# One chunk of w4 loaded by two DMA engines instead of sixteen, in a decode step that streams its cache

## The chip, the cores and the metric

The kernel runs on one core of a Trainium2 chip. The core has TensorE (PE; its weight loads are listed as PEld), VectorE (DVE), ScalarE (ACT), GpSimd (POOL) and SyncE (SP), and sixteen DMA engines that move data between HBM and SBUF, its on-chip memory of 128 partitions. Matmul results go to PSUM. The metric is the time of one execution on the device in microseconds (us); lower is better.

## The reference

Eight sequences, one new token each. Block A is attention over the last 2048 positions of a key and value cache, block B an MLP whose token-shift branch is zero for a sequence of length one:

```python
x = A_x                                                   # [8, 1, 512]
h = x + A(layernorm(x))          # q = x @ wq; softmax(q k^T / sqrt(128)) v; @ wo
# B(u), with u = layernorm(h):
#   x1 = u + 0                   # the shifted branch is zero here
#   B  = x1 + gelu(layernorm(x1) @ w3) @ w4               # w3 [512, 1792], w4 [1792, 512]
h2 = h + B(layernorm(h))
```

There are 8 key-value heads of 128 elements and 32 query heads, all in bf16. Keys and values make 64 MB of the 79 MB that the kernel reads, wq and wo 4 MB each, w3 and w4 1.8 MB each.

## The kernel before

The instruction order of each engine is written out by hand. `Engine.op` appends an operation with the semaphores that it waits for, and `emit` writes the waits and the instructions. `dma` (line 197) appends a transfer; its semaphore gets 16 when the whole transfer has landed. All large loads are issued by SP, in one order: wq, then keys and values in 32 loads of 2 MB through a ring of eight buffers of 16 KB per partition, then wo in four parts, w3 in two, w4 in four. So each transfer stands behind all earlier ones in the queues of the DMA engines, and the order of issue is the order of arrival. A load of keys or values waits until TensorE has read the buffer that it overwrites.

w3 and w4 reuse two buffers of the ring (`w3_sb`, `w4_sb`). w3 goes as two loads of 256 rows with 7 KB per partition (line 669 on). w4's 1792 rows are 14 chunks of 128 rows (`FC = 14`); a chunk is what one matmul contracts over, and its 128 rows stand on the 128 partitions. The loop at line 675 loads 8, 3, 2 and 1 chunks with one DMA each, on four semaphores. In a DMA of r chunks, partition p gets r consecutive rows of 512 elements (r KB in one run), so chunk i of it holds rows `f0 + i`, `f0 + i + r`, and so on. The list `w4_chunks` keeps that as a slice with step r. The same slice picks the columns of w3 in `pe_w3` (line 705), so that row p of the product `y_ps` is what meets row p of w4's chunk. Its inner matmul (line 710) makes one chunk, 128 columns of w3, from one of four 128-row pieces (`kc`) of the contraction. Chunks 0 to 7 lie in one PSUM bank with 64 columns each, chunks 8 to 13 in another with 32 each.

The end of the kernel runs so. When the last part of wo has landed, TensorE finishes the attention's projection (line 548). VectorE and TensorE take the statistics of the layernorms (lines 685 to 700). `pe_w3` runs in two halves, each behind its half of w3. VectorE scales the product (line 738), ScalarE applies gelu (line 741). `pe_fin` (line 747) puts the residual into the output's PSUM tile, and `pe_w4` (line 755) adds w4's chunks, two matmuls per chunk, in four calls; each waits for its part of w4. Two copies (lines 775 and 776) take the result to SBUF, and SP stores it (line 779). `stream` (line 596) puts matmuls that nothing reads between these steps.

Of the kernel before, what the change touches and what calls it, by code (L numbers as in the profile page):

```python
# [12 lines left out]
D = 512  # L13
# [10 lines left out]
KC = D // 128  # L24
# [43 lines left out]
def bass_sequential_preLN__sliding_block_cached__mixer_s_mlp__decode_kernel(  # L68
# [23 lines left out]
    with es:  # L92
# [31 lines left out]
        w3_sb = ring[:, W3S, 0:KC * F].rearrange("p (k f) -> p k f", k=KC)  # L124
        w4_sb = ring[:, W4S, 0:FC * D].rearrange("p (k n) -> p k n", k=FC)
# [45 lines left out]
        uT = P4_sb[:, 0:64, :].rearrange("p (n w) k -> p n (w k)", n=KC)  # L171
# [22 lines left out]
        sem_w4 = [S(f"sem_w4{i}") for i in range(4)]  # L194
        PE, AC, DV, PO, SP = (Engine(S(n)) for n in ("s_pe", "s_act", "s_dve", "s_pool", "s_sp"))

        def dma(eng, dst, src, sem, *waits):
            def f(e):
                e.dma_start(dst, src).then_inc(sem, 16)  # L199
            eng.op(f, *waits, inc=False)  # L200
# [18 lines left out]
        e = DV.op(lambda e: e.bn_stats(st6[:, :], x_sb[:, :]), X)  # L219
        e = DV.op(lambda e: e.bn_aggr(mv[:, :], st6[:, :]), e)  # L220
        e = AC.op(lambda e: e.activation(rstd[:, :], mv[:, 1:2], ACT.Sqrt, bias=eps1[0:B, :], scale=1.0), e, e_eps)
        e = DV.op(lambda e: e.reciprocal(rstd[:, :], rstd[:, :]), e)
# [36 lines left out]
        e = PE.op(pe_xT, e_xln, e_idb)  # L259
# [22 lines left out]
        e = PE.op(pe_qT, *e_qr)  # L282
# [218 lines left out]
        cols = [slice(256 * a + r, 256 * (a + 1), 2) for a in range(2) for r in range(2)]  # L501
# [3 lines left out]
        def bc(t):  # L505
            a = t[:, :]
            return bass.AP(tensor=a.tensor, offset=a.offset, ap=[a.ap[0], [0, KC], [1, B]])
# [47 lines left out]
        at = {4 * (w + 1) + 2: w for w in range(SHARE)}  # L555
# [97 lines left out]
        for l in loads:  # L653
            what, b, j = l
            if what == "wo":
                n, qh = b, QH // NWO
# [4 lines left out]
            n = place[l]  # L661
# [6 lines left out]
        w_free = [taken[quads[n - NS]] for n in (len(quads), len(quads) + 1)]  # L668
# [2 lines left out]
                B_w3[256 * a:256 * (a + 1), :].rearrange("(p r) f -> p (r f)", r=2), sem, w_free[0])  # L671

        FH = 8
        w4_chunks, w4_ends, f0 = [], [], 0
        for r, sem in zip((8, 3, 2, 1), sem_w4):
            lo = len(w4_chunks)
            w4_chunks += [slice(f0 + i, f0 + 128 * r, r) for i in range(r)]
            dma(SP, w4_sb[:, lo:lo + r, :].rearrange("p r n -> p (r n)"),
                B_w4[f0:f0 + 128 * r, :].rearrange("(p r) n -> p (r n)", r=r), sem, w_free[1] if lo == 0 else None)
            w4_ends.append(lo + r)  # L680
            f0 += 128 * r
        assert len(w4_chunks) == FC
# [20 lines left out]
        y_ps, NY = [kbank[0], kbank[2]], (64, 32)  # L703

        def pe_w3(half, lo, hi, *waits):
            def f(e):
                for fc in range(lo, hi):
                    n, f = divmod(fc, FH)
                    for kc in (2 * half, 2 * half + 1):
                        ins = e.matmul(y_ps[n][:, f * NY[n]:(f + 1) * NY[n]], w3_sb[:, kc, w4_chunks[fc]],  # L710
                                       uT[:, kc, 0:NY[n]], start=(kc == 0 and f == 0), stop=(kc == KC - 1),
                                       skip_group_check=True)
                return ins
            return PE.op(f, *waits)
        pe_w3(0, 0, FC, e_u, (sem_w3[0], 16), e_scale[LAST, 1], e_acc[NV - 2])
# [3 lines left out]
        e = AC.op(lambda e: e.activation(s2[:, :], vsum[:, :], ACT.Sqrt, bias=eps2[:, :], scale=(1.0 + EPS) / D), e_vs)  # L719
# [3 lines left out]
        e = DV.op(lambda e: e.reciprocal(r1[:, :], s1[:, :]), e1)  # L723
        e = DV.op(lambda e: e.tensor_tensor(v3(xb[:, :]), v3(hc[:, :]), bc(r1), ALU.mult), e, e_hc)
        e = DV.op(lambda e: e.tensor_tensor(xb[:, :], xb[:, :], hp[:, :], ALU.add), e)
        e = DV.op(lambda e: e.tensor_tensor(v3(fin[:, :]), hT, v3(xb[:, :]), ALU.add), e)
        e = DV.op(lambda e: e.tensor_copy(f_hi[:, :], fin[:, :]), e)
        e_fin = DV.op(lambda e: e.tensor_tensor(f_lo[:, :], fin[:, :], f_hi[:, :], ALU.subtract), e)

        def bcf(t, n):  # L730
            a = t[:, :]
            return bass.AP(tensor=a.tensor, offset=a.offset, ap=[a.ap[0], [0, n], [1, B]])

        e_gT = []
        for n in range(2):
            fn = (FH, FC - FH)[n]
            cs = slice(n * FH * B, (n * FH + fn) * B)
            e = DV.op(lambda e, n=n, cs=cs, fn=fn: e.tensor_tensor(v3(g_x[:, cs]), 
                y_ps[n][:, 0:fn * NY[n]].rearrange("p (f w) -> p f w", w=NY[n])[:, :, 0:B], bcf(r2, fn),
                                                                   ALU.mult), e_y[n], e_r2)  # L740
# [10 lines left out]
        def pe_w4(lo, hi, *waits):  # L751
            def f(e):
                for fc in range(lo, hi):
                    for a in range(2):
                        ins = e.matmul(z_ps[64 * a:64 * a + B, 0:256], gT[:, fc * B:(fc + 1) * B],  # L755
                                       w4_sb[:, fc, 256 * a:256 * (a + 1)].rearrange("p (j r) -> p r j", r=2),
                                       start=False, stop=(fc == FC - 1), tile_position=(0, 64 * a), skip_group_check=True)
                return ins
            return PE.op(f, *waits)
# [7 lines left out]
        PE.op(pe_fin, e_fin, e_exp[LAST], e_scale[LAST, 1])  # L767
        stream(2)
        for n, hi in enumerate(w4_ends):
            e_z = pe_w4(w4_ends[n - 1] if n else 0, hi, (sem_w4[n], 16), e_gT[0 if hi <= FH else 1])  # L770
        e_out = []
        for a in range(2):
            src = z_ps[64 * a:64 * a + B, 0:256].rearrange("p (r j) -> p r j", r=2)
# [39 lines left out]
```

## Time and profile before

| | |
|---|---|
| median of 3 runs | 193.51 us (193.48 to 193.56) |
| profiled execution | 193.76 us, of which the span from first to last instruction is 192.3 us |
| busy share: PE, DVE, ACT, POOL | 83%, 54%, 44%, 19% |
| DMA traffic | 79.18 MB read from HBM, 412 GB/s over the span |
| loads issued by SP | 43: wq 4096 KB, 32 of 2048 KB, 4 of 1024 KB, 2 of 896 KB, and w4's 1024, 384, 256 and 128 KB |
| instruction loads | 16 of 16 KB on queue 8, beside a few of 8 KB on queue 14 |
| granted TensorE clock | full speed throughout |

The profile is of one execution. Its slices of the span give busy shares in tenths. The chain of waits is followed back from the last instruction, at each step to what released it. The table by window gives, for each engine, busy microseconds and the number of instructions, then the clock, the mean busy share of the DMA engines and what they moved. Beside the page, the trace holds the packets of the DMA engines with their queue, start, duration and size, and, for each load, the time of the increments that its semaphore took. It does not number the DMA engines. Times are counted from the start of the span.

### The profile page before, as it was taken

The page shows a single profiled execution, that of the slowest core. Times are in us where ns is not written, and L with a number is a line of the kernel's source. Part 1 is how long each engine was busy: PE and PEld are TensorE (multiplying, and loading weights), DVE is VectorE, ACT ScalarE, POOL GpSimd, SP SyncE. Part 2 cuts the span into 40 slices and gives each one's busy share as a digit, 9 for nine tenths or more (in the row PEclk, how much of TensorE's full clock was granted, in tenths as well). Part 3 has the DMA queues.
Part 4 walks back from the last instruction along what each step waited for, and adds up shares of the span by engine and source line. Part 5 has one row for each costly group of instructions (what it writes and reads, how often), then busy time and mean ns, then how long its engine had stood idle before and what let it go on. Part 6 is the DMA issues. An engine that isn't in the chain of part 4 may idle for free.

```text
span 192.3 us, 4741 instructions
## 1 busy us (share of the span) xinstructions
PE 159.8 (83%) x2108; PEld 101.8 (53%) x2108; DVE 103.8 (54%) x256; ACT 84.4 (44%) x102; POOL 35.8 (19%) x44
## 2 busy tenths in 40 slices
PE   0028999789998989998999797979998998898795
PEld 0015767567665555655656464646565653366472
DVE  7702656367457654665475546554765456552050
ACT  5002776946744544454444532454445423530040
POOL 8000000350520080008000800052004402400000
PEclk9999999999999999999999999999999999999999
DMA  6999999999999999999999999999999999999992
GB/s 220 436 423 436 433 416 433 426 428 423 436 429 433 429 433 423 426 429 431 433 423 433 429 433 429 429 433 426 424 426 429 429 433 433 423 416 430 418 381 77
DMA packets 6244, 79.47 MB, mean 413 GB/s; under 512 B 705, under 2 KB 849, under 8 KB 1361
## 3 DMA queue, kind: packets, MB, share of 16 engines
q1 hardware_dynamic: 6208, 79.18, 97.0%
q8 instruction: 16, 0.26, 0.5%
q10 hardware_dynamic: 16, 0.01, 0.0%
q14 instruction: 4, 0.02, 0.0%
HBM read 79.18 MB, written 0.01 MB: 412 GB/s over the span
## 4 chain that ended last, share of the span: by engine, by line
DMA 78%; PE 16%; DVE 2%; SPq 2%; issue 1%; ACT 0%
DMA ring<-in_A_k_cache_dram 63%; DMA ring<-in_B_w_dram 16%; PE kT_ps L325 8%; PE O_ps L445 3%; PE S_ps L345 3%; SPq L199 2%; DVE kT_sb L336 1%; PE sm L394 1%; PE sm L496 1%; DVE pT_sb L407 1%; PE S_ps L755 0%; DVE mcol L356 0%; ACT P_sb L775 0%; PE sm L360 0%; PE sm L370 0%
## 5 line engine op out<-in xcount | busy, mean ns | idle before, releaser
L334 ACT ACTIVATE kT_sb<-kT_ps 128x1024 bf16<-128x1024 bf16 x64 | 65.2, 1023 | 65.4 <-PE kT_ps L325 65.4
L325 PE MATMUL kT_ps<-ident_p,ring 128*128 128x128 bf16 x1024 | 68.3, 220 | 9.0 <-DMA ring<-in_A_k_cache_dram 7.6
L336 DVE COPY kT_sb<-kT_ps 128x1024 bf16<-128x1024 bf16 x64 | 44.3, 692 | 48.9 <-PE kT_ps L325 48.9
L325 PEld LDWEIGHTS kT_ps<-ident_p,ring 128*128 128x128 bf16 x1024 | 57.7, 98 | 22.5 <-DMA ring<-in_A_k_cache_dram 10.5
L384 POOL TENSOR_TENSOR P_sb<-P_sb,mask_b 128x512 bf16<-128x512 bf16 x30 | 31.2, 1070 | 129.2 <-ACT P_sb L374 120.1
L445 PE MATMUL O_ps<-ring,pT_sb 128*64 128x512 bf16 x208 | 31.6, 390 | 0.0
L345 PE MATMUL S_ps<-kT_sb,qwin 128*32 128x512 bf16 x256 | 26.0, 390 | 0.0
L345 PEld LDWEIGHTS S_ps<-kT_sb,qwin 128*32 128x32 bf16 x256 | 6.8, 93 | 16.3 <-issue 14.4
L394 PE MATMUL sm<-ident_s,P_sb 128*128 128x128 bf16 x120 | 11.6, 219 | 2.0 <-DVE pT_sb L407 0.7
L407 DVE COPY pT_sb<-sm 128x512 bf16<-128x512 bf16 x28 | 11.6, 415 | 1.1 <-PE sm L394 1.1
L445 PEld LDWEIGHTS O_ps<-ring,pT_sb 128*64 128x64 bf16 x208 | 7.7, 108 | 6.1 <-issue 1.6
L394 PEld LDWEIGHTS sm<-ident_s,P_sb 128*128 128x128 bf16 x120 | 7.7, 97 | 4.5 <-issue 3.6
L480 DVE SCALAR_TENSOR_TENSOR acc<-O_ps,own_f,acc 128x128 f32<-128x128 f32 x24 | 8.4, 350 | 0.8
L268 PE MATMUL S_ps<-wbig,xlnT 128*32 128x512 bf16 x32 | 3.4, 596 | 5.3 <-DMA wbig<-in_A_wq_dram 5.3
L374 ACT ACTIVATE P_sb<-S_ps,negcol 128x512 bf16<-128x512 f32 x8 | 5.5, 687 | 3.0 <-DVE negcol L373 3.0
L254 PE MATMUL sm<-ident_b,xln_b 8*128 8x8 bf16 x4 | 0.3, 174 | 7.6 <-DVE xln_b L223 7.6
L496 PEld LDWEIGHTS sm<-sum_f,acc 128*128 128x128 f32 x20 | 3.0, 188 | 6.3 <-DVE pT_sb L407 3.3
L356 DVE TENSOR_REDUCE mcol<-S_ps 128x1 f32<-128x512 f32 x8 | 5.5, 689 | 1.5 <-PE S_ps L345 1.5
L480 DVE SCALAR_TENSOR_TENSOR iota_f<-O_ps,own_f,iota_f 128x128 f32<-128x128 f32 x15 | 5.2, 348 | 1.5 <-ACT iota_f L483 1.2
L596 PE MATMUL O_ps<-kT_sb,ident_b 128*128 128x512 bf16 x21 | 5.8, 379 | 0.0
L435 DVE TENSOR_TENSOR oT_all<-sm,rL 128x16 bf16<-128x16 f32 x15 | 3.4, 229 | 4.4 <-PE sm L496 4.3
L719 ACT ACTIVATE s<-vsum,eps 128x8 f32<-128x8 f32 x1 | 0.3, 301 | 11.8 <-DVE vsum L699 11.8
(123 smaller groups left out, 109.8 us busy)
## 6 DMA issues: line engine op xcount, KB each, us to landing
ring<-in_A_k_cache_dram SPq DMA_DIRECT2D x16, 2048.0 KB, 30.7
ring<-in_A_v_cache_dram SPq DMA_DIRECT2D x16, 2048.0 KB, 26.8
wbig<-in_A_wq_dram SPq DMA_DIRECT2D x1, 4096.0 KB, 12.3
wbig<-in_A_wo_dram SPq DMA_DIRECT2D x4, 1024.0 KB, 29.9
ring<-in_B_w_dram SPq DMA_DIRECT2D x2, 896.0 KB, 34.9
ring<-in_B_w_dram SPq DMA_DIRECT2D x1, 1024.0 KB, 32.1
ring<-in_B_w_dram SPq DMA_DIRECT2D x1, 384.0 KB, 30.3
ring<-in_B_w_dram SPq DMA_DIRECT2D x1, 256.0 KB, 30.5
```

What stands on the lines that cost most here:

```text
L325: ins = e.matmul(kT_ps[m % 3][:, c * 128:(c + 1) * 128], ring[:, s, n * DH:(n + 1) * DH], ident_p[:, :], is_transpose=True)
L334: e_lo[i] = AC.op(lambda e: e.activation(kT_sb[:, i % NKT, 0:1024], kT_ps[2 * i % 3][:, :], ACT.Copy), e_Tlo[i], e_QK.get(i - NKT))
L336: e_hi[i] = DV.op(lambda e: e.tensor_copy(kT_sb[:, i % NKT, 1024:2048], kT_ps[(2 * i + 1) % 3][:, :]), e_Thi[i], e_QK.get(i - NKT))
L345: ins = e.matmul(S_ps[b % 2][32 * h:32 * (h + 1), :], qwin[:, b, 4 * j + h, w0:w0 + 32], kT_sb[:, i % NKT, :].rearrange("p (c h k) -> p h ...
L356: e_max[b] = DV.op(lambda e: e.tensor_reduce(mcol[:, :], S_ps[b % 2][:, :], AX.X, ALU.max), e_QK[8 * b + 7], e_mT.get(b - 1))
L374: e_exp[b] = AC.op(lambda e: e.activation(P_sb[:, :], S_ps[j][:, :], ACT.Exp, bias=negcol[:, j:j + 1], scale=1.0, accum_out=lcol[:, j:j + 1]),
L384: e_sp[b, r] = eng.op(lambda e, r=r, pb=pb, mb=mb: e.tensor_tensor(P4_sb[:, 128 * r:128 * (r + 1), :], pb, mb, ALU.mult), e_exp[b], e_PT.g ...
L394: ins = e.matmul(buf[:, x * 128:(x + 1) * 128], P4_sb[:, 32 * c:32 * (c + 1), :].rearrange("p k h -> p (k h)"), ident_s[:, :], is_transpos ...
L407: e_pT[b, r] = DV.op(lambda e: e.tensor_copy(dst, pT_ps[:, :]), e_PT[b, r], free)
L445: ins = e.matmul(bank(w)[64 * t:64 * (t + 1), :], pT_sb[:, b % NB3, c, 64 * j:64 * (j + 1)], ring[:, s, :].rearrange("p (a c d) -> p c a d ...
L480: e_part[w] = eng.op(lambda e: e.scalar_tensor_tensor(dst, src, own, dst, ALU.mult, ALU.add), e_part[w], e_PV[4 * w + 3])
L596: ins = e.matmul(O2_ps[:, :], ident_b[:, :], kT_sb[:, (NG - 1) % NKT, 0:512], start=True, stop=True)
```

## The change

w4's first chunk gets a DMA of its own. Its source is given as two interleaved halves: 64 even rows, then 64 odd ones, which go to partitions 0 to 63 and 64 to 127, one row of 1 KB to a partition. The outermost dimension of that source has size two, and this DMA is carried by two of the DMA engines. It shares the first of w4's semaphores with the next load, so the first wait in `pe_w4` is for 32. The other 13 chunks are loaded in groups of 7, 3, 2 and 1.

Since partition p of chunk 0 now holds row 2p for p below 64 and row 2(p - 64) + 1 above, `pe_w3` makes this chunk with two matmuls for each `kc`: the 64 even columns of w3 into rows 0 to 63 of the PSUM tile, the 64 odd ones into rows 64 to 127. All else is as before.

```diff
         FH = 8
-        w4_chunks, w4_ends, f0 = [], [], 0
-        for r, sem in zip((8, 3, 2, 1), sem_w4):
+        few = B_w4[0:128, :]
+        dma(SP, w4_sb[:, 0, :], bass.AP(tensor=few.tensor, offset=few.offset, ap=[[D, 2], [2 * D, 64], [1, D]]), sem_w4[0], w_free[1])
+        w4_chunks, w4_ends, f0 = [None], [], 128
+        for r, sem in zip((7, 3, 2, 1), sem_w4):
             lo = len(w4_chunks)
             w4_chunks += [slice(f0 + i, f0 + 128 * r, r) for i in range(r)]
             dma(SP, w4_sb[:, lo:lo + r, :].rearrange("p r n -> p (r n)"),
-                B_w4[f0:f0 + 128 * r, :].rearrange("(p r) n -> p (r n)", r=r), sem, w_free[1] if lo == 0 else None)
+                B_w4[f0:f0 + 128 * r, :].rearrange("(p r) n -> p (r n)", r=r), sem)
...
                     for kc in (2 * half, 2 * half + 1):
-                        ins = e.matmul(y_ps[n][:, f * NY[n]:(f + 1) * NY[n]], w3_sb[:, kc, w4_chunks[fc]],
-                                       uT[:, kc, 0:NY[n]], start=(kc == 0 and f == 0), stop=(kc == KC - 1),
-                                       skip_group_check=True)
+                        parts = [(slice(0, 128), w4_chunks[fc], None)] if fc else [
+                            (slice(64 * a, 64 * (a + 1)), slice(a, 128, 2), (0, 64 * a)) for a in range(2)]
+                        for to, cols, at in parts:
+                            ins = e.matmul(y_ps[n][to, f * NY[n]:(f + 1) * NY[n]], w3_sb[:, kc, cols], uT[:, kc, 0:NY[n]],
+                                           start=(kc == 0 and f == 0), stop=(kc == KC - 1), skip_group_check=True,
+                                           **({} if at is None else dict(tile_position=at)))
...
-            e_z = pe_w4(w4_ends[n - 1] if n else 0, hi, (sem_w4[n], 16), e_gT[0 if hi <= FH else 1])
+            e_z = pe_w4(w4_ends[n - 1] if n else 0, hi, (sem_w4[n], 16 if n else 32), e_gT[0 if hi <= FH else 1])
```

## The prediction

> **What bounds the kernel now.** I read the slices of the span first, then the chain that ended last, then the last microseconds by window.
>
> ```profile
> DMA  6999999999999999999999999999999999999992
> GB/s 220 436 423 436 433 416 433 426 428 423 436 429 433 429 433 423 426 429 431 433 423 433 429 433 429 429 433 426 424 426 429 429 433 433 423 416 430 418 381 77
> ```
>
> The DMA engines are busy from the second slice to the last but one: the kernel streams 79 MB and computes beside it. So what counts is when the last byte lands and what follows. The chain of waits, in order of time, ends so:
>
> ```profile
> 159.31 30.47 DMA ring<-in_B_w_dram
> 189.78 0.04 issue
> 189.82 0.61 PE S_ps L755 x6
> 190.43 0.02 issue
> 190.45 0.45 ACT P_sb L775
> ```
>
> The last transfer is w4's last chunk, landed at 189.78. Behind it stand six matmuls, a copy and the store. The timeline tells how tight that is:
>
> ```profile
> 187.28 0.61 PE L596 MATMUL O_ps<-kT_sb,ident_b 128*128 128x512 bf16 x2
> 187.99 0.77 PEld L755 LDWEIGHTS S_ps<-ring,gT 128*8 128x8 bf16 x16 [0.59 <-DMA ring<-in_B_w_dram]
> ...
> 189.20 0.21 PEld L755 LDWEIGHTS S_ps<-ring,gT 128*8 128x8 bf16 x6 [0.44 <-DMA ring<-in_B_w_dram]
> 189.82 0.09 PEld L755 LDWEIGHTS S_ps<-ring,gT 128*8 128x8 bf16 x4 [0.41 <-DMA ring<-in_B_w_dram]
> 190.13 0.09 PEld L755 LDWEIGHTS S_ps<-ring,gT 128*8 128x8 bf16 x2 [0.22 <-DMA ring<-in_B_w_dram]
> ```
>
> w4's four parts (8, 3, 2, 1 chunks) land at 187.63, 188.85, 189.47 and 189.78, and TensorE starts each of the last three 0.35 us after its landing, having waited 0.22 to 0.44 us. Transfers set the end. But not all transfers:
>
> ```profile
> 185.00:186.00 1.00, 0.64 (x8) 0.43 (x8) 0.81 (x5) 0.89 (x1) 0.00 (x0) 1.00 1.00 410
> 186.00:187.00 1.00, 1.00 (x27) 0.97 (x27) 0.23 (x1) 0.00 (x0) 0.00 (x0) 1.00 0.81 323
> 187.00:188.00 1.00, 0.90 (x13) 0.29 (x14) 0.21 (x1) 0.50 (x2) 0.00 (x0) 1.00 0.59 227
> 188.00:189.00 1.00, 1.00 (x16) 0.61 (x16) 0.00 (x0) 0.00 (x0) 0.00 (x0) 1.00 0.50 185
> ```
>
> The last two columns are the busy share of the 16 DMA engines and GB/s. From 186.4 on about half of the engines have nothing left. The trace keeps the sixteen completion increments of each load, one for each DMA engine. Those of w4's last part are at 186.36, 186.45, 186.45, 186.60, 186.60, 186.79, 187.12, 188.02, and then 189.30, 189.32, 189.35, 189.40, 189.42, 189.60, 189.61, 189.78. Eight engines are late by 3 us. Why:
>
> ```profile
> q8 instruction: 16, 0.26, 0.5%
> q14 instruction: 4, 0.02, 0.0%
> ```
>
> Sixteen instruction loads of 16 KB run between 24.2 and 186.7 us. From one 2 MB load to the next, each of them puts one increment back by 1.1 to 1.5 us; by the end eight engines were hit twice, and the other eight never. Three 8 KB loads (39.9, 88.1, 134.3) put two of the early engines back by 0.7 to 0.9 each: once (187.12) and twice (188.02).
>
> **The change, part by part.** *Bytes off every engine.* One chunk of 128 rows (1 KB each) leaves the load that all sixteen share: 8 packets of 8 KB become 8 of 7 KB. w4's old first part shows 309 ns for an 8 KB packet, w3 shows 272 ns for 7 KB: 8 x 37 = 0.30 us less on each engine. The eight late ones would end at 189.48 instead of 189.78.
>
> *Bytes onto two.* Two engines get 64 rows each. w4's last part is also 1 KB rows: 46 ns a packet, one started every 42 ns. 64 x 42.3 = 2.71 us. The trace shows no DMA confined to two engines and no rows spread over 64 partitions by one engine, so from both sides: below, 42 ns, since no 1 KB packet of these streams starts faster; above, 84 ns, if such an engine shares its target with another stream (below). I take 42: same size, tensor and target. If the two are early engines with leads like 186.36 to 187.12, they end between 186.36 - 0.30 + 2.71 = 188.77 and 187.12 - 0.30 + 2.71 = 189.53. So the end goes to 189.48 or 189.53: 0.25 to 0.30 earlier; I take 0.28.
>
> Which two? The 8 rows of x went as eight 1 KB packets, each squeezed between two packets of an engine's big stream; followed on from there, these engines are, as far as the packets can be told apart, the eight that no 16 KB instruction load hits. A DMA with fewer than sixteen shares, the nearest thing here to the new one, thus went to early engines. [...]
>
> *Issue on SP.* SP blocks when an engine's queue is full: the six issues took 435 to 11,009 ns, and after a blocked one about 85 records (packets and completions) were outstanding on the slowest engine. The new DMA puts 65 on two engines, so SP holds in it until these have only w3 left (85 - 65 = 20 records), near 177.5; the four issues behind it follow as 9 records drain each (2.4 us on w3's 272 ns packets, then 0.4 us): about 179.9, 182.3, 183.1 and 183.5. The early engines run out of w3 at 182.0, the late ones at 185.2, so w4 is there in time. Nobody else waits for SP until the store at 190.99. If this cover fails, an early engine idles inside its 3 us.
>
> *TensorE.* Chunk 0 of w3 becomes two 64-column matmuls per kc: four more pairs, two in each half of L710. 28 of them take 1.45 us, so 2 x 52 ns = 0.10 in each. The first half's lies before a 0.36 us wait for w3. The second moves everything to w4 by 0.10: w4's first matmul at 188.09 instead of 187.99, 16 at 53 ns end at 188.94, the next part could start at 188.90 (188.85 - 0.30 + 0.35), and the third at 189.52. So 0.26 us later TensorE waits again: nothing. Changing between whole and 64-column tiles is bounded by 0, as L747 to L596 (187.07 to 187.28) shows no gap, and by 0.2, which that slack covers. The first part now waits for two DMAs; on the two engines it completes near 187.0 to 187.6, before TensorE is free.
>
> Sum: the profiled execution took 193.76 (span 192.3 and 1.46 around it), 0.25 over the median. 193.76 - 0.28 = 193.48; on the median's scale 193.51 - 0.28 = **193.23**. A measurement here tells about 0.2% (0.39 us) from no change, so this forecast counts as no change.
>
> **Rivals.** *1. Two streams into the same partitions share a rate (slower).* Sixteen engines each feed their own eight partitions at 16 KB in 607 ns, 27 GB/s, without a gap. In the change two engines write all 128 partitions while the other fourteen stream into them. If what saturates is the partitions' side, each 1 KB costs up to 84 ns: 64 x 84 = 5.38, ending at 186.45 - 0.30 + 5.38 = 191.53, 1.75 late; half-way, 63 ns, it is 190.2, 0.4 late. It decides from about 47 ns (engine at 187.12) or 57 ns (186.45). For it: packets of 16 KB at exactly 611 ns whatever else runs, which fits a hard limit on either side. Against: six of x's eight rows, written to eight partitions beside the full stream, took 45 to 56 ns (two others 248 and 348). Time 193.9 to 195.3. [...]
>
> *2. One of the two is the early engine that is already 1.66 behind.* 188.02 - 0.30 + 2.71 = 190.43, 0.65 late: 194.16. Two of eight taken blindly hold it 1 in 4 times.
>
> *3. The two are late engines.* 189.30 to 189.78 - 0.30 + 2.71: 191.7 to 192.2, so 195.4 to 195.9. Against it: x's packets.
>
> *4. It doesn't do what it says:* the source is taken as plain rows and all sixteen engines carry it. Then each engine has the same bytes: 193.5.
>
> *5. More than the 8 KB.* The last increment (189.78) stands 0.17 behind the one before it and seems to be the engine that the instruction load at 186.7 hit. With eight more TensorE instructions that load may fall elsewhere: 0.46 earlier, 193.05.
>
> **Chances.** Forecast 0.42 (same). Rival 1 0.25 (0.01 of it same); rival 2 0.15; rival 3 0.06; rival 4 0.05 (same); rival 5 0.07 (faster). Faster 0.07, same 0.48, slower 0.45. The range runs from 193.1 to 194.9: it leaves out rival 5, rival 3 and the dear end of rival 1. The likeliest case's own range is 193.1 to 193.4.
>
> **What would show it.** Right: the sixteen increments of the last part keep eight late ones, at 189.1 to 189.5; two of the early ones move to 188.8 to 189.5; the 64-row packets start every 42 ns; TensorE's last wait stays near 0.2. Rival 1: those packets take 55 to 84 ns, and two increments stand alone at the end. Rival 2: one stands alone, near 190.4. Rival 3: no packet moves to the early group. Wrong altogether would be a last part whose transfers start late, because SP released it late.

## The result, and the profile after

| | before | after |
|---|---|---|
| median | 193.56 us (193.35 to 193.71, 19 executions) | 194.71 us (193.60 to 195.12, 19 executions) |
| ratio of the means | | 1.0047, 95% interval 1.0032 to 1.0062 |
| profiled execution | 193.76 us, span 192.3 | 193.60 us, span 192.3 |

The change made the kernel slower by half a per cent. The times of the changed kernel fall into two groups with nothing between: 8 executions from 193.60 to 194.09, 11 from 194.69 to 195.12. The profiled one is the fastest, so its trace shows the lower group; a trace of the upper group comes with the first experiment. Lines of the changed kernel stand five further down from the new load on (L710 is now L715, L755 is L760).

Two clocks run through this text. The views count from the start of the span. The times of landings, increments, DMA packets and SP's issues that are given in sentences and in the table near the end, here and in the prediction, were taken from the trace with a zero that lies 0.31 us later. So w3's landing at 185.82 below is the 186.13 at which the DMA of the chain ends. Durations and differences are the same on both.

The slices of the span, DMA share and GB/s, of the kernel after:

```profile
DMA  6999999999999999999999999999999999999992
GB/s 220 436 433 429 429 426 426 429 428 426 433 423 436 429 436 426 423 423 431 429 436 429 426 436 426 433 429 419 428 429 426 433 433 433 426 411 427 420 350 109
```

The last two slices read 350 and 109 where they read 381 and 77. The DMA engines are as busy as before and move less: bytes were put off, and the first row does not show it. The windows of the last microseconds, with clock, DMA share and GB/s at the end:

```profile
183.00:184.00 1.00, 1.00 (x13) 0.54 (x13) 0.90 (x7) 0.00 (x0) 0.00 (x0) 1.00 1.08 398
184.00:185.00 1.00, 1.00 (x26) 0.88 (x24) 0.67 (x4) 0.95 (x3) 0.00 (x0) 1.00 0.99 323
185.00:186.00 1.00, 0.19 (x1) 0.00 (x0) 0.76 (x4) 0.82 (x1) 0.00 (x0) 1.00 1.04 352
186.00:187.00 1.00, 0.83 (x16) 0.79 (x17) 0.00 (x0) 0.00 (x0) 0.00 (x0) 1.00 0.88 343
187.00:188.00 1.00, 1.00 (x27) 0.80 (x26) 0.43 (x2) 0.39 (x2) 0.00 (x0) 1.00 0.63 257
188.00:189.00 1.00, 1.00 (x14) 0.50 (x14) 0.00 (x0) 0.10 (x1) 0.00 (x0) 1.00 0.68 267
```

The first of the two windows from 184 to 186 was, before:

```profile
184.00:185.00 1.00, 1.00 (x25) 0.91 (x23) 0.69 (x5) 0.89 (x3) 0.00 (x0) 1.00 0.96 399
```

From 184 to 186 the engines are full (0.99, 1.04) and move 323 and 352 GB/s; before, these windows moved 399 at a share of 0.96 and 410 at 1.00. Full engines that move less have slower packets, and the packets show it. The two 64-row streams begin at 181.92 and 182.30, as soon as their engines run out of w3, and start a packet every 42 ns until 183.9, then every 45 to 50. From 183.1 to 185.6 the packets of all engines are stretched: 7 KB from 272 ns to as much as 359, 3 KB from 121 to 153 on average, 1 KB from 46 to 54. No 7 KB packet that starts between 184 and 185 takes less than 335 ns.

The timeline of TensorE says who suffers. The first line is of before, the other two are of after:

```profile
185.57 1.45 PE L710 MATMUL kT_ps<-P_sb,ring 128*128 128x64 bf16 x28 [0.36 <-DMA ring<-in_B_w_dram]
184.81 0.38 PE L596 MATMUL O_ps<-kT_sb,ident_b 128*128 128x512 bf16 x1
186.17 1.01 PE L715 MATMUL kT_ps<-P_sb,ring 128*64 128x64 bf16 x16 [0.98 <-DMA ring<-in_B_w_dram]
```

w3's second load lands at 185.82 instead of 185.22, and TensorE, which waited 0.36 us for it, waits 0.98. The weight loads of the end, which the prediction read for its waits:

```profile
188.37 1.11 PEld L760 LDWEIGHTS S_ps<-ring,gT 128*8 128x8 bf16 x22 [0.42 <-DMA ring<-in_B_w_dram]
189.78 0.09 PEld L760 LDWEIGHTS S_ps<-ring,gT 128*8 128x8 bf16 x4 [0.30 <-DMA ring<-in_B_w_dram]
190.08 0.09 PEld L760 LDWEIGHTS S_ps<-ring,gT 128*8 128x8 bf16 x2 [0.20 <-DMA ring<-in_B_w_dram]
```

TensorE now starts w4 at 188.37 (187.99 before) and takes 22 of the 28 in one piece, where it used to stop after 16: when the group of 3 has landed, it is itself still behind. The chain that ended last has changed hands accordingly:

```profile
150.25 35.88 DMA ring<-in_B_w_dram
186.12 0.04 issue
186.17 1.41 PE kT_ps L715 x30
187.58 0.32 PE S_ps L752 x8
187.91 0.54 PE O_ps L596 x2
188.44 1.94 PE S_ps L760 x28
190.38 0.02 issue
190.40 0.45 ACT P_sb L780
```

Before, it ran from a landing of w4 (189.78 in the view) through six matmuls. Now it runs from w3's second landing through TensorE without a gap, 4.2 us of matmuls. w4's last increment, at 189.73, is 0.05 earlier than before and was forecast 0.25 to 0.30 earlier. The sixteen increments of w4's last part are at 186.51, 186.64, 186.82, 186.87, 186.93, 188.79, and ten from 189.33 to 189.73: the eight late engines, and the two that carried 64 rows more. Instruction loads are again 16 on queue 8, with 3 on queue 14 (4 before).

### The profile page after: what moved, and what is told of

Its sections match the earlier page's. It is cut to its first block, busy times and chain, and to the rows that moved or that the text cites. A ratio compares the mean times of both kernels' runs of the same rounds, so it can differ in the third digit from the quotient of the medians.

```text
span 192.3 us, 4750 instructions
## 1 busy us (share of the span) xinstructions
PE 162.6 (85%) x2112; PEld 104.7 (54%) x2112; DVE 103.4 (54%) x256; ACT 84.6 (44%) x102; POOL 35.8 (19%) x44
## 4 chain that ended last, share of the span: by engine, by line
DMA 56%; PE 34%; DVE 4%; ACT 2%; SPq 2%; issue 1%
DMA ring<-in_A_k_cache_dram 31%; DMA ring<-in_B_w_dram 19%; PE kT_ps L325 18%; DMA wbig<-in_A_wq_dram 6%; PE S_ps L345 5%; PE O_ps L445 4%; DVE kT_sb L336 3%; SPq L199 2%; PE S_ps L268 2%; ACT kT_sb L334 1%; PE S_ps L760 1%; PE sm L394 1%; PE sm L496 1%; PE kT_ps L715 1%; ACT L374 1%
## 5 line engine op out<-in xcount | busy, mean ns | idle before, releaser
L325 PE MATMUL kT_ps<-ident_p,ring 128*128 128x128 bf16 x1024 | 70.7, 224 | 5.8 <-DMA ring<-in_A_k_cache_dram 4.6
L325 PEld LDWEIGHTS kT_ps<-ident_p,ring 128*128 128x128 bf16 x1024 | 60.3, 101 | 18.7 <-issue 9.0
L596 PE MATMUL O_ps<-kT_sb,ident_b 128*128 128x512 bf16 x21 | 5.8, 379 | 0.0
```

What stands on the lines that cost most here:

```text
L325: ins = e.matmul(kT_ps[m % 3][:, c * 128:(c + 1) * 128], ring[:, s, n * DH:(n + 1) * DH], ident_p[:, :], is_transpose=True)
L596: ins = e.matmul(O2_ps[:, :], ident_b[:, :], kT_sb[:, (NG - 1) % NKT, 0:512], start=True, stop=True)
```

## The experiments

Three questions: what stretches everyone's packets, why the times form two groups, and whether the idea works once both are known. For the first, rival 1 of the prediction says that a stream into partitions which other engines fill costs that stream; the theory that the profile after suggests is that it costs every engine, and that w3's late landing, not w4's, makes the time. Each run's ratio is against the kernel before, run beside it.

**`again`: the changed kernel unchanged**, to see an execution of the upper group.

> The changed kernel once more, unaltered: its 19 times fell into two groups, 193.60 to 194.09 (8) and 194.69 to 195.12 (11), and the one trace at hand is of the first group. Theory: the two engines that carry chunk 0 start it with different delays in different executions, because the instruction loads of an execution fall on other engines; then a trace of the second group shows one or two increments of w4's last part standing alone, about 1.1 us behind the rest, with the chunk's packets still started every 42 to 50 ns. Rival: in the second group the chunk's packets themselves are slow (60 ns and more). Both expect the two groups again, medians near 193.8 and 194.9.

Measured: 194.0 us, six from 193.76 to 194.0 and five from 194.83 to 195.27; ratio 1.0046 (1.0026 to 1.0066). The profiled execution took 194.83. Neither theory holds there: no increment of w4's last part stands alone behind the rest (the late ones lie from 189.31 to 189.87), and the chunk's packets take 53 ns in the stretch. Its windows:

```profile
187.00:188.00 1.00, 1.00 (x25) 0.73 (x24) 0.43 (x2) 0.48 (x2) 0.00 (x0) 0.85 0.67 263
188.00:189.00 1.00, 1.00 (x6) 0.20 (x6) 0.00 (x0) 0.02 (x1) 0.00 (x0) 0.50 0.67 251
189.00:190.00 1.00, 1.00 (x14) 0.57 (x12) 0.00 (x0) 0.00 (x0) 0.00 (x0) 0.50 0.35 124
190.00:191.00 1.00, 1.00 (x12) 0.60 (x10) 0.00 (x0) 0.00 (x0) 0.00 (x0) 0.50 0.00 0
```

The number behind POOL is the granted TensorE clock: 0.85, then 0.50. TensorE ran at half speed for 3.41 us, from about 187.7. The timeline shows what that costs and what stood ahead of it:

```profile
186.08 1.42 PE L715 MATMUL kT_ps<-P_sb,ring 128*64 128x64 bf16 x30 [1.02 <-DMA ring<-in_B_w_dram]
...
187.75 1.03 PE L596 MATMUL O_ps<-kT_sb,ident_b 128*128 128x512 bf16 x2
188.72 2.85 PE L760 MATMUL S_ps<-ring,gT 128*8 128x256 bf16 x28
```

The same 28 matmuls took 1.99 us in the lower group, the two of L596 0.61. TensorE ends at 191.59 instead of 190.38: 1.21 us, about the distance between the middles of the groups (1.14 us in the 19 executions, 1.4 in these 11). What precedes the fall is the wait of 1.02 us for w3. The end does not wait for transfers here: the windows' GB/s run out at 190 while TensorE goes on. The mean granted clock of the other executions fits: of the 16 in the upper groups all have 0.991 or less, of the 14 in the lower ones eleven have 1.00 and three 0.991. One of these three is the profiled execution of the result, and its half-speed window lies at 117.9 us, where it costs nothing.

**`all16`: the split alone.** Chunk 0 has its own DMA, but of plain rows, so that all sixteen engines carry it; the half-chunk matmuls stay.

```diff
-        dma(SP, w4_sb[:, 0, :], bass.AP(tensor=few.tensor, offset=few.offset, ap=[[D, 2], [2 * D, 64], [1, D]]), sem_w4[0], w_free[1])
+        dma(SP, w4_sb[:, 0, :], few, sem_w4[0], w_free[1])
...
-                            (slice(64 * a, 64 * (a + 1)), slice(a, 128, 2), (0, 64 * a)) for a in range(2)]
+                            (slice(64 * a, 64 * (a + 1)), slice(64 * a, 64 * (a + 1)), (0, 64 * a)) for a in range(2)]
```

> Chunk 0 still has a DMA of its own and its 64-column matmuls, but its source is plain rows, so that all sixteen engines carry it, 8 rows each. If confining it to two engines is what costs, both the stretching of the other packets (7 KB in 272 ns, up to 351 in the changed kernel) and the second group of times go, and the time is that of the kernel before, 193.4 to 193.6. If the extra DMA, the wait for 32 or the four more pairs of matmuls cost, it stays 0.2 us or more above.

Measured: 193.62 us in one group (193.43 to 193.79), ratio 1.0004 (0.9995 to 1.0012). 7 KB packets take 272 ns from 182 to 186, w4's last increment is at 189.75. So neither the added DMA nor the half-chunk matmuls cost anything that can be measured.

**`into8`: the streams with another target.** The two engines write partitions 0 to 7 of a buffer that nothing reads.

```diff
-        dma(SP, w4_sb[:, 0, :], bass.AP(tensor=few.tensor, offset=few.offset, ap=[[D, 2], [2 * D, 64], [1, D]]), sem_w4[0], w_free[1])
+        dma(SP, ring[0:8, 2, :].rearrange("p (r n) -> p r n", r=16), bass.AP(tensor=few.tensor, offset=few.offset, ap=[[D, 2], [2 * D, 64], [1, D]]), sem_w4[0], w_free[1], taken[quads[26]])
```

> The two engines read the same rows but write them into 8 partitions (16 KB each) of a free buffer; w4's chunk 0 is not loaded, and its matmuls run on what the buffer held. If the packets of all engines were stretched by writes into all partitions, 7 KB takes 272 ns again throughout, the late engines end near 189.45 and the faster group of times is near 193.3. If the reading of the interleaved 1 KB rows stretches them, they stay at 320 to 350 ns between 183 and 185.5.

Measured: 193.36 us in one group (193.25 to 193.61), ratio 0.9994 (0.9985 to 1.0003). The packets stay at 272 ns from 183 to 185, and the late engines end at 189.40. The same rows in two streams do no harm into this target, so it is the target that does.

**`rows65`: the source.** Each engine reads 64 consecutive rows, 0 to 63 and 65 to 128, in place of every second one.

```diff
-ap=[[D, 2], [2 * D, 64], [1, D]]
+ap=[[65 * D, 2], [D, 64], [1, D]]
```

> The two engines take rows 0 to 63 and 65 to 128, each a contiguous run of 64 KB, instead of even and odd rows of one run; so row 64 of w4 is left out and the rows of chunk 0 meet other rows of the product. Writes are as in the changed kernel. If the interleaved reading stretches the packets, 7 KB falls back to 272 ns; if the writes into all partitions do, it stays at 320 to 350 ns, and the times are those of the changed kernel, 193.6 to 195.1.

Measured: 194.49 us (193.95, 194.07, 194.91, 194.99), ratio 1.005 (1.0031 to 1.0068). The stretch stays (329, 352 and 315 ns), w3 lands at 185.93, and TensorE waits 1.05 us. Interleaved reading is not the cause.

**`warm` and `cold`: the two groups.** `warm` is the changed kernel with four filler matmuls in place of one between the halves of `pe_w3`; `cold` is the kernel before without the filler there and behind the second statistics matmul. `cold` has no change in any transfer.

```diff
 warm, from the kernel after:
-        stream(1)
+        stream(4)
 cold, from the kernel before:
-        stream(2)
+        stream(0)
...
-        stream(1)
+        stream(0)
```

> The changed kernel with four filler matmuls instead of one between the two halves of w3's product, so that TensorE waits some 0.3 us for w3's second load instead of 1.0. The traces of the changed kernel show that wait at 0.98 and 1.02 us, and in the one of the slower group TensorE's granted clock is 0.5 from 187.4 us on, for 3.41 us. Theory: the clock falls because TensorE stood idle too long; then the slower group of times goes and all lie between 193.6 and 194.1. Rival: the clock falls for another cause (the load of the DMA engines, the power of the chip); then both groups stay, with medians near 193.8 and 195.1.

> The kernel before, w4 in groups of 8, 3, 2, 1, without the filler matmul between the halves of w3's product (0.38 us) and without the two behind the second statistics matmul (0.60 us). No DMA is changed. TensorE then waits about 0.75 us for w3's second load and 0.4 us more ahead of the first half. If idle time of TensorE alone makes the clock fall, a slower group of times appears about 1.1 us above 193.5, in a part of the executions; if it takes the two-engine DMA, all stay at 193.4 to 193.8.

Measured, `warm`: 193.94 us, ten from 193.71 to 194.09 and one at 194.43, no upper group; ratio 1.0015 (1.0006 to 1.0023). The stretch is as in the changed kernel (328, 351, 313 ns) and w3 lands at 185.97; TensorE's idle stretch is 0.38 us, and its clock is full. Ten of the eleven executions have a mean clock of 1.00, the one at 194.43 has 0.991. `cold`: 194.12 us, 193.58 to 194.84, spread out without a clear gap, each with a mean clock of 0.991 or less; ratio 1.0025 (1.0013 to 1.0037). Its windows, of an execution at the low end (193.59):

```profile
185.00:186.00 1.00, 0.45 (x7) 0.45 (x8) 0.76 (x4) 0.81 (x1) 0.00 (x0) 0.67 1.01 415
186.00:187.00 1.00, 1.00 (x27) 0.96 (x26) 0.22 (x1) 0.00 (x0) 0.00 (x0) 0.50 0.87 342
187.00:188.00 1.00, 0.67 (x11) 0.41 (x10) 0.21 (x1) 0.50 (x2) 0.00 (x0) 0.50 0.50 199
188.00:189.00 1.00, 1.00 (x9) 0.38 (x10) 0.00 (x0) 0.00 (x0) 0.00 (x0) 0.62 0.52 193
```

The clock is at half from about 185.34 to 188.76, at 415 GB/s and with w3 on time; TensorE had waited 0.29 and 0.34 us, and the fall lies within its wait of 0.60 us for w3. So the fall came with idle time of TensorE and no change of transfers, and with filler (`warm`) it stayed away in ten of eleven executions. Where the half-speed stretch fell decided the price: in `cold` it ended 0.29 us after w4's first matmul (188.47), whose 28 took 1.87 us; in `again` it lay over them, and they took 2.85. `warm` also leaves the stretch by itself: 0.15%, about 0.3 us.

**`into64`: crowding.** As `into8`, into partitions 0 to 63 with two rows each, so that both engines walk the half of the partitions that one of them had.

```diff
-        dma(SP, w4_sb[:, 0, :], bass
+        dma(SP, ring[0:64, 2, 0:1024], bass
```

> The two engines read the same rows and write them into partitions 0 to 63 of a free buffer, 2 KB each; w4's chunk 0 is not loaded, and its matmuls run on what the buffer held. Into 8 partitions nothing was stretched (7 KB in 272 ns), into all 128 every engine's packets were (up to 352 ns). If the stretch is a matter of the partitions written to, only the engines that feed partitions 0 to 63 are stretched, and if these are the eight early ones the late ones end near 189.45 and the faster times are near 193.3. If many short pieces to many partitions stretch everybody, 7 KB stands at 320 to 350 ns for the late engines too, and the times are those of the changed kernel.

Measured: 194.93 us (194.11, 194.66, 195.19, 195.21), ratio 1.0062 (1.0043 to 1.008). 7 KB packets take 358, 426 and 352 ns in the three windows from 183 on, 1.57 times as long in the middle one; the window from 184 moves 275 GB/s. Half the partitions, more stretch, for all packets alike (402 ns is the shortest that starts between 184 and 185).

**`own2`: eight engines in place of two.** 256 rows of w4 go to partitions 0 to 63, four rows each, by eight DMAs of eight partitions; the other chunks in groups of 6, 3, 2 and 1. The two filler matmuls ahead of w4's product are left out.

```diff
+        for i in range(8):
+            ps = slice(32 * (i // 4) + i % 4, 32 * (i // 4) + 32, 4)
+            dma(SP, w4_sb[ps, FC - NO:NSL, :].rearrange("p r n -> p (r n)"), own[ps, :], sem_w4[0], w_free[1])
```

> A whole kernel of another kind, from the kernel before: 256 rows of w4 (two chunks) go to partitions 0 to 63 alone, 4 rows (4 KB) each, by eight DMAs of 8 partitions, so that eight engines carry them and each writes partitions that it feeds anyway; the other twelve chunks in groups of 6, 3, 2, 1; the 256 rows are contracted as four half chunks of 64 rows; no filler ahead of w4's product. If the eight engines are the early ones and nothing is stretched, the late engines lose 16 KB each, 0.6 us: the last increment near 189.2, TensorE's wait for it stays, and the time is near 193.0. If these DMAs fall on the late engines, they end 0.6 us later, near 194.1. If writing into half of the partitions stretches others, it is 193.3 to 193.6.

Measured: 194.9 us in two groups (194.09 to 194.27, 195.54 to 195.71), ratio 1.006 (1.0036 to 1.0084). No stretch: 7 KB stay at 272 ns, and w3 lands on time. But the last increments are at 185.86 twice, five at 187.03 to 187.96, seven at 188.56 to 189.18, and two at 189.99 and 190.25. By these, two engines of the early half got nothing of the extra load, and two of the late half carried a share of it. TensorE waited 1.15 us for w4's first part, and its clock fell to 0.50 in the profiled execution. So 256 KB went to partitions 0 to 63 beside the full stream without a stretch, where the 128 KB of `into64` took the packets to 426 ns. That is as if each engine wrote only partitions that it fed anyway, though the trace, which does not number the engines, can't tell. But this way bytes went to engines that had no time.

**`late`: the streams behind everything.** The changed kernel with the two-engine load issued last and counted with the group of 2, so that it can't meet w3.

> The changed kernel with the two-engine load issued last, behind the groups of 7, 3, 2 and 1, and counted with the group of 2; TensorE multiplies its chunk together with that group's. The two streams then begin when their engines have carried all their other parts, at about 186.5, end about 189.2, and lie beside w4's last groups, no longer beside w3's second load. Theory one (the stretch of all engines' packets comes with many partitions written by two engines, and w3's second load, not the two streams, made the kernel slower): w3's second load lands at 185.2 as before the change, TensorE waits about 0.4 us ahead of its second half, the clock does not fall, and the times form one group without those near 195. What comes of w4's end depends on the stretch: if packets stretch to 1.25 times from 187.0 to 189.2 as they did from 183.1 to 185.6, the ten late engines end at 189.8 to 190.0, the two streams at 189.7, and the time is 193.5 to 193.9. Theory two (the packets stretch only while all sixteen engines are busy and the whole passes about 400 GB/s: with five early engines already done, there is room): the late engines end at 189.5 with packets of 272 ns, and the time is 193.2 to 193.35, faster than before. Against both: if the group near 195 stays, w3's load is not what makes it.

```diff
-        dma(SP, w4_sb[:, 0, :], bass.AP(tensor=few.tensor, offset=few.offset, ap=[[D, 2], [2 * D, 64], [1, D]]), sem_w4[0], w_free[1])
...
+        dma(SP, w4_sb[:, 0, :], bass.AP(tensor=few.tensor, offset=few.offset, ap=[[D, 2], [2 * D, 64], [1, D]]), sem_w4[2])
         assert len(w4_chunks) == FC
```

Measured: 193.65 us in one group (193.52 to 193.95), ratio 1.0009 (1.0 to 1.0018). w3 lands at 185.21, nothing stretches before 187, and hardly anything after: of the 65 packets of 2 KB that start between 187 and 189, 53 take 84 ns as ever, and nine of the others stay below 135. Their means of 94 and 91 ns come mostly from three single packets of 227 to 231 ns. These are two streams of the same rows into the same partitions in the same order as in the changed kernel, but the DMA engines as a whole are busy to 0.71 and 0.60 here (windows from 187 and 188). So target and order alone don't make the stretch; in these runs it came only beside a full stream, as theory two had it. w4's last increment is at 189.48, the forecast's number to the hundredth, and still nothing is gained; that the time lies in theory one's range has another reason. The chain shows it:

```profile
172.46 17.25 DMA ring<-in_B_w_dram
189.71 0.04 issue
189.75 0.64 PE S_ps L760 x8
190.39 0.02 issue
```

Eight matmuls stand behind the landing of the group of 2 (189.71 in the view, 189.78 before), where before six did: chunk 0 was counted with that group. The lead of the transfers went into TensorE's queue. But the group near 195 is gone, as it must be if w3's late landing makes it.

**`into8far`: whose partitions.** `into8` with partitions 120 to 127 in place of 0 to 7.

```diff
-        dma(SP, ring[0:8, 2, :].rearrange
+        dma(SP, ring[120:128, 2, :].rearrange
```

> The earlier run in which the two engines wrote 8 partitions of a buffer that nothing reads, with partitions 120 to 127 in place of 0 to 7; chunk 0 of w4 is again not loaded, so its product is left out in effect. Theory one (what stretches everyone's packets is the number of partitions that two engines write, 64 or more against 8): no packet is stretched, 7 KB stay at 272 ns, time 193.2 to 193.5 in one group. Theory two (it is that they write partitions which other engines feed; 0 to 7 happened to be near to the two engines' own): the 7 KB packets take 320 to 430 ns between 183 and 186, w3's second load lands 0.6 to 1.3 us late, and times near 195 come back.

Measured: 196.78 us (196.26 to 197.35), ratio 1.018 (1.0164 to 1.0196). The windows, the first line that of `into8` for comparison:

```profile
184.00:185.00 1.00, 1.00 (x27) 0.92 (x25) 0.69 (x5) 0.94 (x3) 0.00 (x0) 1.00 0.98 400
183.00:184.00 1.00, 0.47 (x3) 0.00 (x0) 0.84 (x7) 0.11 (x1) 0.00 (x0) 1.00 1.17 305
184.00:185.00 1.00, 0.71 (x14) 0.70 (x15) 0.71 (x4) 0.98 (x3) 0.00 (x0) 1.00 0.95 193
185.00:186.00 1.00, 0.94 (x21) 0.63 (x19) 0.63 (x4) 0.68 (x1) 0.00 (x0) 1.00 1.02 206
```

Two engines of sixteen, with 128 KB in all, halve what the core reads (193 GB/s at a DMA share of 0.95) for more than three microseconds. Every 7 KB packet that starts between 184 and 186 takes 2.0 to 2.1 times 272 ns. Eight partitions in both runs, so it is not their number: with the two streams into partitions 0 to 7 the packets kept their 272 ns in that window, into 120 to 127 they took 560.

**`spread`: the same partitions in another order.** The load of the changed kernel cut into four, so that each engine steps by four partitions and not by one.

```diff
-        dma(SP, w4_sb[:, 0, :], bass.AP(tensor=few.tensor, offset=few.offset, ap=[[D, 2], [2 * D, 64], [1, D]]), sem_w4[0], w_free[1])
+        for j in range(4):
+            dma(SP, w4_sb[j:128:4, 0, :], bass.AP(tensor=few.tensor, offset=few.offset + 2 * j * D, ap=[[D, 2], [8 * D, 16], [1, D]]), sem_w4[0], w_free[1])
...
-(sem_w4[n], 16 if n else 32)
+(sem_w4[n], 16 if n else 80)
```

> The changed kernel with the two-engine load cut into four, each of 32 partitions: partitions j, j+4, j+8, ..., for j = 0 to 3. Every row lands in the same partition and is multiplied in the same way; only the order in which each engine walks its 64 partitions changes, from one partition to the next to steps of four. [...] The earlier runs differ in how long the two streams stay near one place: 128 partitions in order stretched the 7 KB packets to 272 x 1.29 ns, 64 partitions with two rows each to x 1.57, partitions 120 to 127 to x 2.05, and partitions 0 to 7 not at all. [...] Theory two (a row written into a partition that another engine feeds costs a fixed surplus, in whatever order): the stretch stays at 1.25 to 1.3, w3 lands at 185.7 to 185.9, and times near 195 stay.

Measured: 193.41 us in one group (193.26 to 193.63), ratio 0.9992 (0.9983 to 1.0001). The same rows reach the same partitions in two streams, and 1.3 us of the changed kernel's median are gone. A fixed surplus in whatever order, theory two's, is not what was measured. Windows, and the last lines of the chain:

```profile
184.00:185.00 1.00, 1.00 (x26) 0.91 (x24) 0.68 (x4) 0.98 (x3) 0.00 (x0) 1.00 0.97 370
185.00:186.00 1.00, 0.33 (x5) 0.12 (x4) 0.66 (x4) 0.71 (x1) 0.00 (x0) 1.00 1.07 411
```

```profile
180.52 8.99 DMA ring<-in_B_w_dram
189.51 0.04 issue
189.56 0.61 PE S_ps L761 x6
190.17 0.02 issue
```

370 and 411 GB/s against 323 and 352. From 183 to 185 the 7 KB packets take at most 1.12 times as long (theory two: 1.25 to 1.3), the streams' own 1 KB packets 46 ns as alone. w3 lands at 185.53 (theory two: 185.7 to 185.9), TensorE waits 0.67 us, and the chain is again w4's landing with six matmuls behind it, 0.26 us earlier than before the change.

Side by side, the mean of 7 KB packets (ns) in the windows from 183, 184 and 185 on; the column of GB/s is from the views:

| run | partitions written by two engines | 7 KB packets | 1 KB at 184 | GB/s at 184 | w3 lands | ratio |
|---|---|---|---|---|---|---|
| `all16` | nothing apart | 272, 272, 272 | 46 | 406 | 185.48 | 1.0004 |
| `into8` | 0 to 7 | 272, 272, 286 | 46 | 400 | 185.29 | 0.9994 |
| `spread` | 0 to 127, steps of 4 | 295, 291, 296 | 46 | 370 | 185.53 | 0.9992 |
| after | 0 to 127 in order | 329, 351, 298 | 54 | 323 | 185.82 | 1.0047 |
| `into64` | 0 to 63, two rows each | 358, 426, 352 | 66 | 275 | 186.28 | 1.0062 |
| `into8far` | 120 to 127 | 526, 560, 558 | 87 | 193 | 187.69 | 1.018 |

One packet of some 760 ns beside an instruction load is in the 286 of `into8` and in the 296 of `spread`. w3's landing differs by 0.27 us between traces without any stretch (185.21 in `late`, 185.48 in `all16`), so only the larger delays in that column tell something. What fits the runs is a limit on the side of the partitions; this is the author's estimate, and its sum is made here for two of them. One engine undisturbed brings 7168 B in 272 ns, 26.4 GB/s, to its partitions. In `into8far` an engine gets 7168 B in 560 ns, 12.8 GB/s, and each stream 25.5 / 2 packets of 1 KB per us, 13.1 GB/s: together 25.9, as if one stream and one engine shared what one engine has. In `spread` the 7 KB packets of 183.4 to 184.2 take 1.105 times as long, 23.8 GB/s, and 2 x 24.1 GB/s of streams, if they fall evenly on what the sixteen engines write, are 3.0 more for each: 26.9. Both sums, from the packet rows, come near the 26.4 of one engine. Which partitions belong together, the runs bound but don't map, and why 0 to 7 took the two streams at 272 ns they don't show. That all packets slow down together, in `into8far` each one of 7 KB that starts between 184 and 186 to 2.0 to 2.1 times, the runs show and do not explain.

## Why the prediction was wrong, point by point

The interval of the forecast, 193.1 to 194.9, holds the median, and so does rival 1's 193.9 to 195.3. Both are luck: neither has the way through w3 and the clock by which the time came about. The likeliest case, 193.23 and a little faster, did not come.

*Bytes off every engine, 0.30 us:* right. Where packets are stretched little or not at all the late engines end at 189.40 (`into8`), 189.48 (`late`) and 189.52 (`spread`); forecast 189.48.

*Bytes onto two, 42 ns a packet:* right for the first 1.6 to 1.9 us of the streams, 45 to 54 ns after. Both went to early engines; rivals 2, 3 and 4 did not happen. But the reason given for it, that x's eight packets went to the eight engines that no instruction load hits, did not carry over to `own2`: of the engines that took its DMAs of eight partitions, two were late ones by the increments.

*The eight late ones would end at 189.48:* **this step failed.** It took the other fourteen engines' packets as fixed at 272 ns while two streams wrote over all 128 partitions. Rival 1 looked at the right place, the partitions written (272 ns with 0 to 7, 560 with 120 to 127, window from 184), with the wrong victim: it charged the streams up to 84 ns a row and let everyone else go free. In the trace the streams pay 54, and the price is up to 1.29 times on all packets over some 2.5 us: 0.25 us of the 0.30 given back at w4's end, and w3 0.6 us late. The rival's own test, two increments alone at the end, did not show; ten stand together.

*TensorE at nothing:* **failed as well, and this is the larger part.** The matmuls do cost nothing (`all16`). But the 0.26 us of slack was counted from w4's landing, with w3's held at 185.22. With w3 at 185.82 the slack is used up and the chain runs through TensorE; in more than half of the executions its clock falls too. Lower group: 193.77 in the middle, 0.2 over before. Upper group: another 1.1. A clock of 1.00 in every window of before was taken for a constant; in `cold`, with a wait of 0.60 us for w3 in place of 0.36 and 0.29 and 0.34 us ahead of it, it fell to 0.50.

*The last landing:* misread, without effect on the sum. The prediction put the 189.78 of the chain, which is on the views' clock, beside its own list, where w4's last part ends at 189.78 too. On the views' clock the four parts land at 187.94, 189.16, 189.78 and 190.09. TensorE starts each of the last three 0.04 us after its landing (189.20, 189.82, 190.13) and not 0.35; and the six matmuls stand behind the group of 2, while two stand behind the last chunk. As its whole list is shifted alike, the differences that the sum is made of hold.

*SP's issue:* wrong in its working, without effect. The new DMA held SP for 0.64 us (155.47 to 156.11) and not until 177.5; the group of 3 held it 16.5 us, to 179.97, and the last two were out at 180.9. No part started late, so the test for "wrong altogether" did not apply.

*The sum:* with the failed term mended by the order of the rows, `spread`, w4 lands 0.26 us earlier, as the forecast had it (0.25 to 0.30), and the time is 193.41, with a ratio whose interval just includes 1. The forecast's gain of 0.28 us would be a ratio of 0.9986, and that lies in the interval as no gain at all does. So it is shown that `spread` beats the changed kernel, and open whether it beats the one before.

What brings the clock down stays open in part. The record of the clock shows a grid: in each trace with a fall inside the kernel, the stretch at full speed ahead of it lasted a whole number of 3.413 us (170.67 us, 50 of them, in `again` and `own2`; 163.84, 48, in `cold`; 167.25, 49, in `into8far`; 95.57, 28, in the changed kernel's own trace; 102.40, 30, in `spread`), and it began at 15.8 to 22.3 us, in each execution at another time. Why some points of the grid brought a fall and others none the runs don't tell; the busy share of TensorE in the 3.41 us ahead of the point does not by itself divide them. Ahead of a fall, TensorE was busy for 2.39 of 3.41 us in `again` (184.28 to 187.69) and 2.38 in `cold`, 70%, but for 3.06 in `own2`, 90%. The 3.41 us from 116.01 in `again` had 1.76 us, 52%, and no fall. The changed kernel's own trace has its 0.98 us wait almost whole in those from 182.72 (2.47 us, 72%), and no fall either. So with idle time added at the end the clock fell (`again`, `cold`) and with filler in its place it did so in one execution of eleven at most (`warm`); which amount is enough the runs don't show.

## What to carry to other kernels

Before giving bytes to engines that have time, ask which partitions they will write and who is writing there. Full DMA share with falling GB/s was the sign here (0.99 at 323 GB/s, where the kernel before had 0.96 at 399), and late were the loads that ran beside the moved one: w3 by 0.60 us. If rows must be written beside other engines' streams, try another order: steps of four partitions took the stretch from 1.29 times to at most 1.12 from 183 to 185. The same rows late, beside engines that are no longer all busy (0.71), stretched hardly anything (`late`). And count slack from every landing that the chain could pass through, with the clock as something that a wait of one microsecond can take away (1.02 us in `again`, then a clock of 0.50).

## What the runs showed of the hardware

- Two engines writing 128 KB into partitions 120 to 127 while a full stream arrived cut the whole core's transfers from 400 to 193 GB/s in the window from 184; into partitions 0 to 7 they left the packets at 272 ns there and the time at 193.36 us; in steps of four over all 128, packets took up to 1.12 times as long from 183 to 185. In order over all 128, they stretched packets up to 1.3 times beside a full stream and hardly at all when the DMA engines were busy to 0.71 and less (`late`, 53 of 65 packets of 2 KB at 84 ns).
- The stretch began about 1.2 us after the first stream (181.9 to 183.1), and in `into8far` 0.8 to 1.1 us after it. What holds it back so long the runs don't tell.
- TensorE's clock fell to half for 3.41 us after 1.02 us of idle time in the 3.41 us ahead (`again`), also without any change of transfers (`cold`, 1.03 us); with a wait of 0.38 us it did not in the profiled execution of `warm`. The falls came a whole number of 3.413 us after the clock had risen, and 1.65 us of idle time in the 3.41 us from 116.01 of `again` passed without one.
- The engines that carried `own2`'s DMAs of eight partitions were not the eight early ones: by the increments of w4's last part, two of them were late.
